# The opening of a two-problem sliding-window attention kernel: Q and K of the first quarter of x computed block by block

## The chip, the cores and the metric

The kernel runs on one core of one Trainium2 chip. The metric is the device time of one execution in microseconds. The kernel before takes 609.3 us (median of three runs, 609.28 to 609.43).

## The reference, cut to what matters

Two independent problems, A and B, have the same shape: x of 2048 x 1024, weights `wqkv` of 1024 x 3072 and `wo` of 1024 x 1024, 32 heads of width 32, each query seeing the last 256 keys. All data are bf16. The results are put side by side.

```python
qkv = (x @ wqkv).reshape(B, S, 3, H, Dh)          # -> q, k, v
scores = einsum(q, k) * Dh ** -0.5                # masked to 0 <= i - j < 256
o = einsum(softmax(scores), v)
out = o.reshape(B, S, D) @ wo
```

## The kernel before

TensorE needs x with its columns on the partitions. Most of x is transposed by DMA on its way in. The first quarter of A's x (512 rows, four blocks of 128) comes in plain rows, and TensorE transposes it: eight 128x128 transposes to a block, into a bank of PSUM, from which ScalarE copies the first half and VectorE the second half into `xT`. The eight column tiles of x are the eight steps (`ct`) over which a projection accumulates.

The loads of the opening, in the order of issue (the first on ScalarE's queue, the others on SyncE's):

```python
load_wqk(0, 0, nc.scalar)                      # Q weights of the first head group
for a in range(QB):
    nc.sync.dma_start(out=xrow[a], in_=problems[0][0][a * P:(a + 1) * P, :])
    if a == 1:
        load_wqk(0, 1, nc.sync)                # K weights
load_wv(0, 0, CT, nc.sync)
new_x(0, 1)
load_x(0, 1)                                   # the next quarter, transposed by DMA
# ... cut
```

TensorE's part of the opening. `keep_warm` issues filler matmuls on zeros, so that the array's clock is up when the work comes:

```python
warm = ps_proj.tile([P, 512], F32, name="pp")

def keep_warm(n):
    for _ in range(n):
        nc.tensor.matmul(warm[:], lhsT=blank[:, 0:P], rhs=blank[:, 0:512], start=True, stop=True)

keep_warm(6)
flips = [ps_acc.tile([P, 512], F32, name="acc") for _ in range(2)]
# ... cut: a third bank of the score tile, a fourth of ps_acc

def flip(a):                                   # transposes of block a, then the two copies
    # ... cut
    for ct in range(CT):
        nc.tensor.transpose(out=f[:, ct, :], in_=xrow[a][:, ct * P:(ct + 1) * P],
                            identity=ident[:])
    dst = xT[(0, 0)][:, :, a * P:(a + 1) * P]
    half = CT // 2
    nc.scalar.copy(out=dst[:, :half, :], in_=f[:, :half, :])
    nc.vector.tensor_copy(out=dst[:, half:, :], in_=f[:, half:, :])

def first(which, lo):                          # Q (0) or K (1), 256 columns, eight matmuls
    for _, f in qk_steps(0, which, 0, lo, lo + 256, held[which], last=lo > 0):
        f()

flip(0)
keep_warm(4)
flip(1)
keep_warm(3)
first(0, 0)
flip(2)
flip(3)
first(1, 0)
first(0, 256)
first(1, 256)
emit(0, chains[0].size)                        # V of the first two blocks
```

The projections share two PSUM slots (`ps_proj`, `bufs=2`): a new chain (`new_pp`) takes the slot that was used longest ago, and must wait until its contents have been cast to SBUF. The cast of a finished Q or K goes to ScalarE or VectorE, whichever a small model of the engines in the kernel's builder takes to be free first.

Of the kernel before, what the change touches and what calls it, by code (L numbers as in the profile page):

```python
# [9 lines left out]
F32 = mybir.dt.float32  # L10
# [8 lines left out]
P = 128  # L19
# [7 lines left out]
QB = 4  # L27
SLOTS = 4
# [50 lines left out]
def _fast_path(ctx, tc, cfg, problems, outs, consts, certify):  # L79
    nc = tc.nc  # L80
# [36 lines left out]
    ps_st = ctx.enter_context(tc.tile_pool(name="ps_st", bufs=1, space=PSUM))  # L117
    ps_acc = ctx.enter_context(tc.tile_pool(name="ps_acc", bufs=2, space=PSUM))
    ps_proj = ctx.enter_context(tc.tile_pool(name="ps_proj", bufs=2, space=PSUM))
# [6 lines left out]
    blank = top[:].bitcast(BF16)  # L126
# [16 lines left out]
    def load_wqk(g, which, queue, lo=0, hi=CT):  # L143
        pi, t = divmod(g, T)
        queue.dma_start(out=wqk[g][:, lo:hi, which, :],
                        in_=wsrc(pi)[:, lo:hi, which, t * P:(t + 1) * P])
# [18 lines left out]
    def qk_tiles(g):  # L165
        if g not in qks:
            qks[g] = (qkp.tile([P, S], BF16, name="qT"), qkp.tile([P, S], BF16, name="kT"))
        return qks[g]

    def by_columns(out, lo, hi, lhsT, rhs, start, stop):  # L170
        if whole[0]:
            nc.tensor.matmul(out[:, lo:hi], lhsT=lhsT, rhs=rhs, start=start, stop=stop,  # L172
                             skip_group_check=True)
            return
        for c in range(0, P, 32):
            nc.tensor.matmul(out[c:c + 32, lo:hi], lhsT=lhsT[:, c:c + 32], rhs=rhs, start=start,  # L176
                             stop=stop, tile_position=(0, c), skip_group_check=True)
# [4 lines left out]
    def add_or(dst):  # L182
        def f():
            nc.vector.tensor_tensor(out=top[:], in0=top[:], in1=dst.bitcast(I32),
                                    op=ALU.bitwise_or)
        side.append((COST["or"], f, False))

    def evacuate(out, in_, engines=("act", "dve")):
        if clock.evacuate(engines) == "act":
            nc.scalar.copy(out=out, in_=in_)  # L190
        else:
            nc.vector.tensor_copy(out=out, in_=in_)

    def new_pp():
        clock.chain()
        return ps_proj.tile([P, 512], F32, name="pp")

    def qk_steps(g, which, k, lo=0, hi=512, st_=None, last=True):
        pi = g // T
        st_ = {} if st_ is None else st_  # L200
        steps = []
        for ct in range(CT):
            def f(ct=ct):
                if "pp" not in st_:
                    st_["pp"] = new_pp()
                by_columns(st_["pp"], lo, hi, wqk[g][:, ct, which, :], xT[(pi, k)][:, ct, lo:hi],
                           ct == 0, ct == CT - 1)
                clock.pe += NS_MM * (hi - lo) / 512.0
                if ct == CT - 1 and last:
                    dst = qk_tiles(g)[which][:, k * 512:(k + 1) * 512]  # L210
                    evacuate(dst, st_["pp"][:])
                    add_or(dst)
            steps.append((NS_MM * (hi - lo) / 512.0, f))
        return steps
# [192 lines left out]
    def emit(now, budget):  # L407
        done = 0.0
        while (current or chains) and done < budget - 0.5 * (current[0][0] if current else NS_MM):
            if not current and not start_chain(now):  # L410
                break
            ns, f = current.pop(0)
            f()
            done += ns
            if side and (clock.dve < clock.pe + 100.0 or len(side) > 8):
                run_side()
# [129 lines left out]
    load_wqk(0, 0, nc.scalar)  # L546
    for a in range(QB):
        nc.sync.dma_start(out=xrow[a], in_=problems[0][0][a * P:(a + 1) * P, :])
        if a == 1:
            load_wqk(0, 1, nc.sync)  # L550
    load_wv(0, 0, CT, nc.sync)
    new_x(0, 1)
# [8 lines left out]
            new_wv(1)  # L561
            load_wv(1, 0, CT, nc.sync)

    warm = ps_proj.tile([P, 512], F32, name="pp")

    def keep_warm(n):
        for _ in range(n):
            nc.tensor.matmul(warm[:], lhsT=blank[:, 0:P], rhs=blank[:, 0:512], start=True, stop=True)  # L568

    keep_warm(6)  # L570
    flips = [ps_acc.tile([P, 512], F32, name="acc") for _ in range(2)]
    flips = [f[:] for f in flips]
    flips.append(ps_st.tile([P, 4, SLOTS, P], F32, name="st")[:, 0].rearrange("p a q -> p (a q)"))
    flips.append(None)
    held = [{}, {}]

    def flip(a):
        if a == 3:
            flips[a] = ps_acc.tile([P, 512], F32, name="acc")[:]
        f = flips[a].bitcast(BF16).rearrange("p (ct q) -> p ct q", q=P)  # L580
# [5 lines that stand above are left out]
        nc.scalar.copy(out=dst[:, :half, :], in_=f[:, :half, :])  # L586
        nc.vector.tensor_copy(out=dst[:, half:, :], in_=f[:, half:, :])

    def first(which, lo):
        for _, f in qk_steps(0, which, 0, lo, lo + 256, held[which], last=lo > 0):  # L590
            f()

    flip(0)
    keep_warm(4)
    flip(1)
    keep_warm(3)
    first(0, 0)
    flip(2)
    flip(3)
    first(1, 0)  # L600
    first(0, 256)
    first(1, 256)
    emit(0, chains[0].size)

    sealed = first_use(G - 1, NQ - 1, 0)
    for now in range(END):
# [3 lines left out]
        while due and due[0][0] <= now:  # L610
            _, pg, pk = due.pop(0)
# [14 lines left out]
    while due:  # L626
        _, pg, pk = due.pop(0)
# [132 lines left out]
def kernel(  # L760
# [48 lines left out]
    with tc.manual_schedule():  # L809
        with ExitStack() as fctx:  # L810
            _fast_path(fctx, tc, cfg, problems, outs, consts, [reduce_bits, decide])
# [40 lines left out]
```

## Time and profile before

| | before |
|---|---|
| median time | 609.3 us |
| span of the profiled run | 607.6 us |
| TensorE busy | 98% |
| TensorE's share of the chain that ended last | 96% |
| first V matmul, first scores | 11.99, 13.83 us |

Two ways of reading matter here. The chain that ended last is followed backwards from the last instruction, at each step to whatever released it; an engine with 96% of it sets the time. The timeline lists instructions by their start, with repeats of one kind merged into one line ("x8"); in brackets is the idle time of that engine before the line, and what ended it. A merged line hides the pauses inside it, so a line that lasts longer than its matmuls should is a sign of a wait. The lines themselves are in the prediction.

### The profile page before, as it was taken

Reading aid. Unit: us, or ns where it says so; the run is one execution under the profiler, and the core shown is the slowest. Engines: PE = TensorE matmul, PEld = TensorE weight load, DVE = VectorE, ACT = ScalarE, POOL = GpSimd, SP = SyncE. Lnnn points to the kernel's source line nnn. Section 1 sums busy time; section 2 is a strip of 40 time slices with the busy share of each in tenths; the row PEclk is TensorE's granted clock in tenths of the full one; section 3 lists DMA queues with packets and bytes.
Section 4 is the critical chain, followed back from the end, with each engine's and each line's share of the span. In section 5 each row is a group of like instructions: output and inputs, shape, how many; then the busy total and the mean of one; then the engine's idle time right before and its main releaser. Section 6 shows DMA issues by size and latency. Waiting matters only on the chain.

```text
span 607.6 us, 28768 instructions
## 1 busy us (share of the span) xinstructions
PE 593.6 (98%) x12786; PEld 344.3 (57%) x12838; DVE 468.4 (77%) x1199; ACT 441.1 (73%) x376; POOL 326.3 (54%) x630
## 2 busy tenths in 40 slices
PE   8999999999999999999999999999999999999996
PEld 6555466656655756564556756655455665545443
DVE  1677889898898898897888887898888887897200
ACT  3778887788888887877778877777776777785332
POOL 0565666665666666556555565555555655554000
PEclk9999999999999999999999999999999999999999
DMA  9833110111015501442111100112021040113222
GB/s 234 182 92 89 37 38 3 38 38 39 3 38 90 114 14 30 82 101 77 38 37 38 38 4 8 33 37 81 2 68 34 4 106 21 55 58 120 72 79 64
DMA packets 86802, 35.47 MB, mean 58 GB/s; under 512 B 65552, under 2 KB 86160, under 8 KB 86672
## 3 DMA queue, kind: packets, MB, share of 16 engines
q1 hardware_dynamic: 85632, 33.31, 22.2%
q8 instruction: 102, 1.67, 1.2%
q10 hardware_dynamic: 1040, 0.26, 0.2%
q14 instruction: 28, 0.23, 0.1%
HBM read 17.83 MB, written 8.39 MB: 43 GB/s over the span
## 4 chain that ended last, share of the span: by engine, by line
PE 96%; ACT 2%; issue 1%; DMA 1%; ACTq 0%
PE pp L176 44%; PE pp L172 28%; PE acc L513 13%; PE st L451 10%; ACT pt L459 1%; DMA oT<-in_A_x_dram 1%; PE acc L582 0%; PE pp L568 0%; ACT kT L190 0%; ACT vt L190 0%; PE st L582 0%; ACT osb L190 0%; PE pp L805 0%; ACTq L190 0%
## 5 line engine op out<-in xcount | busy, mean ns | idle before, releaser
L459 ACT ACTIVATE pt<-st 128x2048 bf16<-128x2048 f32 x180 | 338.0, 1878 | 91.6 <-PE st L451 73.5
L471 POOL TENSOR_SCALAR_AFFINE_SELECT pt<-pt 128x512 bf16<-128x512 bf16 x224 | 154.5, 690 | 145.7 <-ACT pt L459 143.1
L467 POOL TENSOR_SCALAR_AFFINE_SELECT pt<-pt 128x512 bf16<-128x512 bf16 x256 | 179.2, 701 | 85.8 <-ACT pt L459 85.8
L524 DVE RECIPROCAL rinv<-acc 128x128 f32<-128x128 f32 x128 | 122.0, 953 | 57.0 <-PE acc L513 56.4
L176 PE MATMUL pp<-xT,wqk 128*32 128x512 bf16 x2712 | 163.1, 379 | 0.0
L481 DVE TENSOR_TENSOR both<-pt 128x512 bf16<-128x512 bf16 x224 | 137.1, 651 | 0.0
L176 PEld LDWEIGHTS <-wqk 128*32 128x32 bf16 x2712 | 69.3, 97 | 54.2 <-issue 0.4
L172 PE MATMUL pp<-xT,wqk 128*128 128x512 bf16 (+1 forms) x323 | 76.7, 369 | 4.1 <-issue 2.4
L176 PE MATMUL pp<-wv,xT 128*32 128x256 bf16 x2436 | 75.9, 273 | 0.0
L451 PE MATMUL st<-qT,kT 32*128 32x384 bf16 (+2 forms) x1488 | 71.5, 269 | 0.1
L176 PEld LDWEIGHTS <-xT 128*32 128x32 bf16 x2436 | 63.8, 97 | 6.2
L529 DVE STREAM_SHUFFLE wide<-rinv 128x128 f32<-128x128 f32 x256 | 64.6, 298 | 0.0
L513 PE MATMUL acc<-pt,vt 128*32 128x128 bf16 (+1 forms) x2160 | 63.3, 239 | 0.0
L172 PE MATMUL pp<-wo_sb,oT 128*128 128x512 bf16 (+1 forms) x269 | 59.3, 373 | 1.3 <-issue 0.9
L451 PEld LDWEIGHTS <-kT 32*128 32x128 bf16 x1488 | 22.2, 92 | 64.5 <-issue 63.3
L190 ACT CAST osb<-pp 128x512 bf16<-128x512 f32 (+1 forms) x52 | 30.0, 577 | 39.1 <-PE pp L172 24.4
L531 DVE TENSOR_TENSOR oT<-acc,wide 128x256 bf16<-128x256 f32 x128 | 54.3, 425 | 4.4
L176 PE MATMUL pp<-wo_sb,oT 128*32 128x512 bf16 x952 | 55.6, 379 | 0.0
L172 PEld LDWEIGHTS <-wqk 128*128 128x128 bf16 x362 | 33.4, 98 | 37.0 <-issue 6.8
L172 PE MATMUL pp<-wv,xT 128*128 128x256 bf16 x415 | 50.9, 273 | 1.4 <-ACT kT L190 0.6
L513 PEld LDWEIGHTS <-vt 128*32 128x32 bf16 x2160 | 35.9, 96 | 26.4 <-issue 24.1
L172 PEld LDWEIGHTS <-xT 128*128 128x128 bf16 x415 | 38.9, 98 | 12.0 <-issue 6.1
(46 smaller groups left out, 386.5 us busy)
## 6 DMA issues: line engine op xcount, KB each, us to landing
out_dram<-osb SPq DMA_DIRECT2D x63, 128.0 KB, 1.8
wqk<-in_B_wqkv_dram SPq DMA_DIRECT2D x32, 128.0 KB, 2.5
wqk<-in_A_wqkv_dram SPq DMA_DIRECT2D x24, 128.0 KB, 2.7
wo_sb<-in_A_wo_dram SPq DMA_DIRECT2D x16, 128.0 KB, 2.2
wv<-in_B_wqkv_dram SPq DMA_DIRECT2D x16, 128.0 KB, 2.8
wo_sb<-in_B_wo_dram SPq DMA_DIRECT2D x16, 128.0 KB, 2.4
oT<-in_A_x_dram SPq DMA_DIRECT2D x4, 256.0 KB, 5.4
wv<-in_A_wqkv_dram SPq DMA_DIRECT2D x2, 512.0 KB, 5.9
```

The lines of the kernel that those rows point to most:

```text
L172: nc.tensor.matmul(out[:, lo:hi], lhsT=lhsT, rhs=rhs, start=start, stop=stop, skip_group_check=True)
L176: nc.tensor.matmul(out[c:c + 32, lo:hi], lhsT=lhsT[:, c:c + 32], rhs=rhs, start=start, stop=stop, tile_position=(0, c), skip_group_check=True)
L190: nc.scalar.copy(out=out, in_=in_)
L451: nc.tensor.matmul(st[:, r, a:b, :], lhsT=kT[32 * r:32 * r + 32, j * P:(j + 1) * P], rhs=qT[32 * r:32 * r + 32, q * P:(q + b - a) * P], st ...
L459: nc.scalar.activation(out=pt[:, :, :n, :].rearrange("p r a q -> p r (a q)"), in_=st[:, :, :n, :].rearrange("p r a q -> p r (a q)"), func= ...
L467: nc.gpsimd.affine_select(out=blk, in_=blk, pattern=[[0, 4], [1, P]], compare_op=ALU.is_ge, fill=0.0, base=0, channel_multiplier=-1)
L471: nc.gpsimd.affine_select(out=blk, in_=blk, pattern=[[0, 4], [-1, P]], compare_op=ALU.is_gt, fill=0.0, base=0, channel_multiplier=1)
L481: nc.vector.tensor_tensor(out=both[:, :, h, :], in0=pts[s0][:, :, a0, :], in1=pts[s1][:, :, a1, :], op=ALU.add)
L513: nc.tensor.matmul(acc[32 * r:32 * r + 32, o:o + w_], lhsT=lhsT, rhs=src[:, r, :, :], start=(x == 0), stop=(x == len(moves) - 1), tile_pos ...
L524: nc.vector.reciprocal(out=rinv[:], in_=acc[:, 2 * P:3 * P])
L529: nc.vector.stream_shuffle(out=wide[:, h * P:(h + 1) * P], in_=rinv[:], mask=[16 * h] * 32)
L531: nc.vector.tensor_tensor(out=oTs[(pi, k)][:, t, (p % 2) * 256:(p % 2 + 1) * 256], in0=acc[:, 0:256], in1=wide[:], op=ALU.mult)
```

## The change

The intent is to start Q and K as soon as there is a block to work on, rather than at 7.56 us, and to use that work in place of fillers. Each block, once transposed, is followed by its own 128 columns of Q and K. K's weights must then come earlier, so their load moves ahead of block 1. The fillers write into a bank of the score tile, no longer into a projection slot, and there are two fewer.

```diff
-        if a == 1:
+        if a == 0:
             load_wqk(0, 1, nc.sync)
@@
-    warm = ps_proj.tile([P, 512], F32, name="pp")
+    spare = ps_st.tile([P, 4, SLOTS, P], F32, name="st")[:].rearrange("p r a q -> p r (a q)")
+    warm = spare[:, 1]
@@
-    def first(which, lo):
-        for _, f in qk_steps(0, which, 0, lo, lo + 256, held[which], last=lo > 0):
-            f()
+    def first(a):
+        for which in range(2):
+            for _, f in qk_steps(0, which, 0, a * P, (a + 1) * P, held[which], last=a == QB - 1):
+                f()
 
     flip(0)
-    keep_warm(4)
+    keep_warm(3)
+    first(0)
     flip(1)
-    keep_warm(3)
-    first(0, 0)
+    keep_warm(2)
     flip(2)
+    first(1)
     flip(3)
-    first(1, 0)
-    first(0, 256)
-    first(1, 256)
+    first(2)
+    first(3)
     emit(0, chains[0].size)
```

(The third transposition bank is `spare[:, 0]`, as before under another name.)

More of the change, by code (lines that the diff above doesn't have):

```diff
@@ L562, in _fast_path @@
             load_wv(1, 0, CT, nc.sync)
-    warm = ps_proj.tile([P, 512], F32, name="pp")
+    spare = ps_st.tile([P, 4, SLOTS, P], F32, name="st")[:].rearrange("p r a q -> p r (a q)")
+    warm = spare[:, 1]
     def keep_warm(n):
         for _ in range(n):
-            nc.tensor.matmul(warm[:], lhsT=blank[:, 0:P], rhs=blank[:, 0:512], start=True, stop=True)
+            nc.tensor.matmul(warm, lhsT=blank[:, 0:P], rhs=blank[:, 0:512], start=True, stop=True)
     keep_warm(6)
@@ L572, in _fast_path @@
     flips = [f[:] for f in flips]
-    flips.append(ps_st.tile([P, 4, SLOTS, P], F32, name="st")[:, 0].rearrange("p a q -> p (a q)"))
+    flips.append(spare[:, 0])
     flips.append(None)
```

## The prediction

> **What bounds the kernel now.** I read the page first: busy time by engine, then the chain of work that ended last.
>
> ```profile
> PE 593.6 (98%) x12786; PEld 344.3 (57%) x12838; DVE 468.4 (77%) x1199; ACT 441.1 (73%) x376; POOL 326.3 (54%) x630
> ...
> PE 96%; ACT 2%; issue 1%; DMA 1%; ACTq 0%
> PE pp L176 44%; PE pp L172 28%; PE acc L513 13%; PE st L451 10%; ACT pt L459 1%; DMA oT<-in_A_x_dram 1%; PE acc L582 0%; PE pp L568 0%; ACT kT L190 0%; ACT vt L190 0%; PE st L582 0%; ACT osb L190 0%; PE pp L805 0%; ACTq L190 0%
> ```
>
> TensorE is the bound; the other engines have room. The one DMA in the chain is the first block of x (1%), so the chain runs from that load through TensorE to the end. The change touches only the opening, some 14 of 607.6 us, so I read that from the timeline: start, length, engine, work, and in brackets what ended the idle time.
>
> ```profile
> 1.31 2.74 PE L568 MATMUL pp<-top 128*128 128x512 bf16 x6 [1.31 <-DVE ones L783]
> ...
> 4.34 1.04 PE L582 MATMUL acc<-ident,oT 128*128 128x128 bf16 x8 [0.29 <-DMA oT<-in_A_x_dram]
> ...
> 5.17 1.11 PE L568 MATMUL pp<-top 128*128 128x512 bf16 x4
> 5.42 0.59 ACT L586 COPY xT<-acc 128x512 bf16<-128x512 bf16 x1 [2.84 <-PE acc L582]
> 6.04 0.42 DVE L587 COPY xT<-acc 128x512 bf16<-128x512 bf16 x1 [4.73 <-ACT xT L586]
> ...
> 6.26 0.62 PE L582 MATMUL acc<-ident,oT 128*128 128x128 bf16 x8
> ...
> 6.72 0.81 PE L568 MATMUL pp<-top 128*128 128x512 bf16 x3
> ...
> 7.56 1.06 PE L172 MATMUL pp<-xT,wqk 128*128 128x256 bf16 x8
> ...
> 9.35 2.81 PE L172 MATMUL pp<-xT,wqk 128*128 128x256 bf16 x24
> ...
> 11.32 0.59 ACT L190 CAST qT<-pp 128x512 bf16<-128x512 f32 x1 [1.14 <-PE pp L172]
> ...
> 11.99 1.91 PE L172 MATMUL pp<-wv,xT 128*128 128x256 bf16 x16
> 12.19 0.59 ACT L190 CAST kT<-pp 128x512 bf16<-128x512 f32 x1 [0.29 <-PE pp L172]
> ...
> 13.83 0.40 PE L451 MATMUL st<-qT,kT 32*128 32x384 bf16 x8
> ```
>
> L568 are filler matmuls on zeros that hold the clock up; L582 transposes a 128-row block of x; ScalarE, then VectorE, copy half of it each to xT; L172 are the projections. Two starts matter: V at 11.99 and the first scores at 13.83. After V has started I see no wait of TensorE for a load in the first 40 us: the waits view there lists loads only for the raw x blocks. A later V means a later end by as much.
>
> Even before, TensorE's slack in this stretch is small. From the filler at 5.17 to V at 11.99 (6.82 us) it issues 7 fillers (one per 0.216, the first 0.30: 1.59), 24 transposes (one per 0.056, with a start-up of 0.01: 1.35) and 32 projection matmuls (one per 0.109: 3.49), in all 6.43. Idle is about 0.37: 0.15 for block 1 to land, 0.19 for ScalarE's copy of it, 0.03 for VectorE's half.
>
> **What the Trainium skill says.**
> - "TensorE: Matmul & The Clock Gate", Part 1: the clock is halved until the array has been busy for a window of some 3.4 us, then warm matmuls start every N/2.4 ns + 2.5. The trace agrees: fillers start every 0.43 us at first and every 0.216 from about 5.5 us; transposes go from 0.107 to 0.056. The profile's table by stretch gives a granted clock of 1.00 throughout and doesn't show this.
> - The same page, "Back-to-back issue gap": weight-load and matmul pairs with N=128 sustain about 81 ns each. Here it differs: eight 128-column transposes, each with its own weights, take from 6.26 to 6.72, 0.057 each. I use 0.056.
> - "PSUM — Partial Sum Buffer", "PSUM bank collisions raise a hardware error": two engines may not touch one bank and quadrant at once, reads included. The trace shows the consequence: VectorE's copy starts 0.03 after ScalarE's ends (5.42+0.59, then 6.04), so a block takes 1.04 us from first to last copy.
> - "DMA: Bandwidth & Descriptors", "Queues, rings and completion order": each DMA engine consumes a ring in order. The transfer view agrees at the granularity of these loads: issue plus time to landing gives block 0 at 4.30, Q weights (ScalarE's queue) 5.44, block 1 at 6.22, K weights 7.32, blocks 2 and 3 at 8.00 and 8.73.
>
> **The change part by part.**
> The comparison of instruction orders says that only the opening changes. ScalarE loses the cast of the first kT and VectorE gains it; TensorE has 60 rows more (32 matmuls and 32 weight loads more for Q and K, two fillers with their loads fewer). Behind V all engines carry the same operations in the same order.
>
> *Loads.* K weights go ahead of block 1. Between 5.44 and 7.32 both were delivered, 1.88 us, K taking 1.10 of it. Swapped: K weights land at about 6.5, block 1 at about 7.3; blocks 2 and 3 stay.
>
> *Fillers.* 13 become 11, and behind block 0 there are 5 instead of 7: -0.43 us. They now use a bank of the score tile, so Q and K take the two projection slots; V still takes Q's slot, as before.
>
> *Arithmetic.* 32 matmuls of 256 columns (0.109) become 64 of 128 (0.056): 3.58 for 3.49, +0.09.
>
> *Waits.* I step the new order through with the trace's intervals: a copy starts 0.26 after the last transpose starts; ScalarE 0.59, VectorE 0.42; a waiting matmul starts 0.05 after its copy ends. Times are starts of the first matmul.
> 1. Transposes of block 0 at 4.34, three fillers 5.17 to 5.90. ScalarE's copy ends 6.00: Q of block 0 at 6.06, **idle 0.15**. Its four steps last until 6.28; VectorE's half ends 6.46: **idle 0.24**. Q done 6.74; K (weights 6.5, just in time) done 7.19.
> 2. Block 1 lands at 7.3: transposes at 7.35, **idle 0.16**, done 7.80. Copies 8.00 to 8.59 and 8.62 to 9.05.
> 3. Two fillers to 8.24; transposes of block 2 to 8.68, copied 8.88 to 9.93. Q of block 1: four steps, until 8.91; VectorE's half free at 9.10: **idle 0.19**. Q and K done 9.77.
> 4. Transposes of block 3 to 10.22, copied 10.42 to 11.01 and 11.04 to 11.46. Q and K of block 2 from 10.22 to 11.12 without a wait. Q of block 3 at 11.12, four steps, until 11.34; VectorE's half free at 11.52: **idle 0.18**. Last Q matmul starts 11.69, last K matmul 12.13; TensorE free at 12.19.
> 5. V needs Q's slot. Before, the last Q matmul was eight 256-column K matmuls ahead of the end, and the cast ended at 11.91, just before V. Now only eight of 128 columns lie between. Cast of qT from 11.94 to 12.53, V at 12.58: **idle 0.39**.
>
> *Sum.* Idle is 0.15+0.24+0.16+0.19+0.18+0.39 = 1.31 where it was 0.37: +0.94. With -0.43 and +0.09: **+0.60**. V starts at 12.58 instead of 11.99, scores at 14.42 instead of 13.83. kT, on VectorE, is ready at about 13.1, under V's 1.84 us of matmuls, so its move costs nothing. The intended gain, Q and K at 6.06 instead of 7.56, is real but goes into gaps: the blocks' landings and copies set the pace, and useful work is spread out rather than shortened.
>
> **The rivals.**
> - *The filled gaps win.* Had every wait on a copy a cover, the saving would be at most the fillers and the old idle time less the extra arithmetic: 0.43+0.37-0.09 = 0.7, or 608.6. For it: the first projections start 1.5 us earlier. Against: in step 4 nothing but Q and K of block 3 is left behind the last copy, and V waits for Q's cast. A milder form, with block 1 landing near 7.1 or the cast handed over faster, gives 609.6.
> - *Narrow matmuls pay for weight loads.* At the skill's 81 ns the 64 would take 1.6 us more; some falls into the gaps, so 611. For it: these loads read Q and K weights from another layout. Against: the transposes' 0.056 with the same 128x128 loads.
> - *The clock falls back.* More gaps, two fillers fewer. An estimate: one window of 3.4 us at half speed costs some 1.7 us, 611.6. Against: idle before 9.1 adds up to 0.74 in the 3.4 us since 5.7, no gap over 0.24.
> - *K weights arrive late.* If they landed at 6.9, the stall would only move from block 1's transposes to K's; block 1 lands at 7.3 anyway. About zero.
> - *The delay is swallowed later.* TensorE would have to wait there for something that doesn't move with it. The next block of x lands at 13.95 and is used at 15.92, so there is nothing to swallow.
>
> **Range and chances.** 609.3 + 0.6 = 609.9 us. The landing of block 1 carries 0.15 either way, V's wait 0.2, repeats 0.1; the long tail is on the slow side (clock, weight loads). Range 609.3 to 610.6. Two per cent is 12 us; the stretch changed lasts some 10, and nothing behind it changes. Faster 0.01, within 2% 0.98, slower 0.01.
>
> **What would show it.** In the timeline after: Q matmuls at 6.06 (four, then a gap to 6.5); transposes of block 1 at about 7.35, released by the DMA; gaps near 9.0 and 11.4; V at about 12.6, behind the cast of qT; scores at about 14.4; the span longer by the same 0.6. 128-column projections every 0.056, not 0.081. The chain still TensorE. I am wrong if V starts before 12.0, if block 1 lands by 6.9, if matmuls behind 6 us show cold intervals, or if the scores shift and the span doesn't.

## The result, and the profile after

The changed kernel took 610.14 us in the median (609.52 to 610.54, six runs), the kernel before 609.37 (609.18 to 610.27, six runs, the first three of which gave the 609.3 above). The ratio is 1.0008 with a 95% interval from 0.9995 to 1.0021. A ratio here is the mean time of one kernel's fast runs over that of the other's of the same rounds, so it isn't quite the ratio of the medians quoted. By the runs alone the two kernels are the same within 2%, and even the sign is not certain. The profile is sharper.

The page after, its busy times and the chain that ended last:

```profile
PE 593.9 (98%) x12816; PEld 344.9 (57%) x12868; DVE 469.0 (77%) x1200; ACT 440.6 (72%) x375; POOL 326.3 (54%) x630
...
PE 96%; ACT 2%; issue 1%; DMA 1%; ACTq 0%
```

TensorE has 30 matmuls more and otherwise the picture is the same. The timeline of the opening after (L569 are the fillers, L583 the transposes, L587 and L588 the two copies, L190 and L192 the casts):

```profile
4.29 1.03 PE L583 MATMUL acc<-ident,oT 128*128 128x128 bf16 x8 [0.23 <-DMA oT<-in_A_x_dram]
...
5.11 1.19 PE L569 MATMUL st<-top 128*128 128x512 bf16 x3
...
6.14 1.14 PE L172 MATMUL pp<-xT,wqk 128*128 128x128 bf16 x16
...
7.23 0.62 PE L583 MATMUL acc<-ident,oT 128*128 128x128 bf16 x8
...
7.89 0.58 ACT L587 COPY xT<-acc 128x512 bf16<-128x512 bf16 x1 [1.95 <-PE acc L583]
...
8.51 0.42 DVE L588 COPY xT<-acc 128x512 bf16<-128x512 bf16 x1 [2.11 <-ACT xT L587]
...
8.57 1.25 PE L172 MATMUL pp<-xT,wqk 128*128 128x128 bf16 x16
...
10.10 2.13 PE L172 MATMUL pp<-xT,wqk 128*128 128x128 bf16 x32
...
11.81 0.58 ACT L190 CAST qT<-pp 128x512 bf16<-128x512 f32 x1 [0.93 <-PE pp L172]
...
12.26 0.69 DVE L192 CAST kT<-pp 128x512 bf16<-128x512 f32 x1 [0.92 <-PE pp L172]
12.45 1.91 PE L172 MATMUL pp<-wv,xT 128*128 128x256 bf16 x16 [0.23 <-ACT qT L190]
...
14.29 0.40 PE L451 MATMUL st<-qT,kT 32*128 32x384 bf16 x8
```

Q starts at 6.14 instead of 7.56, yet V starts at 12.45 instead of 11.99 and the first scores at 14.29 instead of 13.83: 0.46 us later. The bracket behind V names the reason nearest to it: TensorE stood waiting for the cast of qT. (The bracket says 0.23 because it counts from the modelled end of the last K matmul. This document counts idle time from start to start: V starts 0.446 behind the last K matmul, where a 128-column matmul is followed after 0.056, so the wait is worth 0.39.) Even a merged line shows pauses: sixteen projections of 128 columns last 1.14 or 1.25 us, against 1.06 where nothing interrupts them (an experiment below has that line).

What the delay becomes later can be read by pairing the 180 groups of score matmuls of the two traces: the first is 0.46 late, the last 0.46, and every one between within a few hundredths. The last matmul of the kernel is 0.46 late too (602.36 instead of 601.89). The span is 0.64 longer; the other 0.18 comes behind the last matmul, where the last store took 3.1 us to land instead of 2.9.

### The profile page after: what moved, and what is told of

Read it like the earlier page. It is cut to its first block, busy times and chain, and to the rows that moved or that the text cites. A ratio compares the mean times of both kernels' runs of the same rounds, so it can differ in the third digit from the quotient of the medians.

```text
span 608.3 us, 28827 instructions
## 1 busy us (share of the span) xinstructions
PE 593.9 (98%) x12816; PEld 344.9 (57%) x12868; DVE 469.0 (77%) x1200; ACT 440.6 (72%) x375; POOL 326.3 (54%) x630
## 4 chain that ended last, share of the span: by engine, by line
PE 96%; ACT 2%; issue 1%; DMA 1%; ACTq 0%
PE pp L176 44%; PE pp L172 28%; PE acc L513 13%; PE st L451 10%; ACT pt L459 1%; DMA oT<-in_A_x_dram 1%; PE acc L583 0%; PE st L569 0%; ACT kT L190 0%; ACT vt L190 0%; ACT qT L190 0%; PE st L583 0%; ACT osb L190 0%; PE pp L807 0%; ACTq L190 0%
## 5 line engine op out<-in xcount | busy, mean ns | idle before, releaser
L190 ACT CAST osb<-pp 128x512 bf16<-128x512 f32 (+1 forms) x52 | 30.0, 576 | 39.1 <-PE pp L172 24.4
```

The source lines that it names most:

```text
L190: nc.scalar.copy(out=out, in_=in_)
```

## The experiments

Ten kernels were run, in three groups on the chip; each had five runs, beside nine of the kernel before for each group. All results were correct. All verdicts on the time are "same" with intervals of about 0.13% to either side, so the readings below come from the profiles. Each profile is one execution. For a fair comparison, the table gives when the transposes of block 1 start, when V starts, and the distance between them: the landing of the loads differs from run to run, and everything behind block 1 moves with it.

| kernel | block 1 | V | distance | scores | span | median (before in the same group) |
|---|---|---|---|---|---|---|
| before | 6.26 | 11.99 | 5.73 | 13.83 | 607.6 | 609.37 |
| after | 7.23 | 12.45 | 5.22 | 14.29 | 608.3 | 610.14 (609.37) |
| r_after | 7.21 | 12.43 | 5.22 | 14.27 | 608.4 | 610.21 (609.70) |
| e1_loads_only | 7.62 | 13.34 | 5.73 | 15.19 | 609.1 | 610.87 (610.11) |
| e2_order_only | 8.16 | 13.37 | 5.21 | 15.21 | 609.1 | 610.48 (610.11) |
| e3_qk_spare | 7.07 | 11.89 | 4.83 | 13.74 | 608.2 | 610.09 (610.11) |
| e4_no_fill | 7.62 | 13.28 | 5.66 | 15.12 | 609.1 | 610.89 (610.11) |
| e5_two_banks | 7.33 | 12.18 | 4.85 | 14.02 | 608.2 | 610.00 (609.70) |
| e6_both | 7.34 | 11.79 | 4.45 | 13.63 | 607.5 | 609.68 (609.70) |
| e7_x_first | 6.64 | 13.95 | – | 15.79 | 609.7 | 610.98 (609.70) |
| e8_x_first_fill | 5.64 | 11.40 | – | 13.24 | 607.5 | 609.77 (609.51) |
| e9_both_fill | 7.14 | 11.61 | 4.46 | 13.45 | 607.2 | 609.48 (609.51) |

Between before and after, block 1 comes 0.97 us later and the distance is 0.51 shorter: together they are the 0.46 by which V is late.

My theory was the prediction's sum: the landing of block 1, the two copies in series and V's wait for the cast of qT cost more than the fillers saved. The rivals were that the loads' order is free, that the wait for the cast only hides another, that the copies' series is not what opens the gaps, and that the clock makes the difference.

**The changed kernel again (r_after).** No edit.

> The changed kernel once more, beside the others, to see how much of its opening repeats. The runs so far have block 0 of x landing anywhere from 4.0 to 4.6 us. My theory: V starts 5.1 to 5.3 us behind the first transpose of block 1, wherever that falls (5.22 in the first profile; 5.73 in the kernel before), and the time is 0.3 to 0.9 us over before. Rival (the difference is chance): another distance, or a time under before.

From the timeline of its opening:

```profile
5.04 0.93 PE L569 MATMUL st<-top 128*128 128x512 bf16 x3
...
5.92 1.29 PE L172 MATMUL pp<-xT,wqk 128*128 128x128 bf16 x16
...
7.21 0.62 PE L583 MATMUL acc<-ident,oT 128*128 128x128 bf16 x8
...
12.43 1.91 PE L172 MATMUL pp<-wv,xT 128*128 128x256 bf16 x16 [0.23 <-ACT qT L190]
```

The distance came out the same to 0.01 us, and the time again above before: ratio 1.0012 (0.9998 to 1.0025). The opening repeats behind block 1. Ahead of it the three fillers were shorter here (0.93 us instead of 1.19) and the projections waited longer (1.29 instead of 1.14), with no effect on V; the section on the prediction comes back to this. The total repeats less well: in this profile TensorE lost a further 0.35 us near 260 us, in one group of eight matmuls (the one against the constant ones) that lasted 0.62 us instead of 0.28, with nothing named as a cause.

**The load order alone (e1_loads_only).** The kernel before, with one line changed:

```diff
-        if a == 1:
+        if a == 0:
             load_wqk(0, 1, nc.sync)
```

> The kernel before, with only the K weights' load moved ahead of block 1 of x; TensorE's order unchanged. My theory (the landings of the blocks set the pace of the opening): block 1 lands at about 7.2 instead of 6.2 us, its transposes start at 7.23 instead of 6.26, and nothing behind them is early, so V starts at about 12.95 (before 11.99), the first scores at 14.8, and the time is 0.9 to 1.0 us over before, some 610.4. Rival (the order of the loads is free, the change's cost lies in the narrow matmuls and copies alone): V stays within 0.1 us of 11.99.

The timeline of its block 1:

```profile
7.62 0.62 PE L582 MATMUL acc<-ident,oT 128*128 128x128 bf16 x8 [1.40 <-DMA oT<-in_A_x_dram]
...
13.34 1.91 PE L172 MATMUL pp<-wv,xT 128*128 128x256 bf16 x16
```

The mechanism was as expected: TensorE waits 1.40 us for block 1, and V follows at the same 5.73 us as in the kernel before. The size wasn't, since in this run all the loads landed 0.3 to 0.4 us later than in the profile after (block 0 at 4.57 us instead of 4.24, block 1 at 7.57 instead of 7.19). So the order of loads is not free, and in the old order of work it is pure loss.

**The order of work alone (e2_order_only).** The changed kernel, with that line put back:

```diff
-        if a == 0:
+        if a == 1:
             load_wqk(0, 1, nc.sync)
```

> The changed kernel with the loads in the order of before (block 1 ahead of the K weights). My theory: the K matmuls of block 0, second in the queue, wait until 7.36 us for their weights, block 1's transposes start at 7.8 although block 1 landed at 6.2, and every later step moves by that: V at about 13.0 (after 12.45), 0.5 to 0.6 us over after, 1.0 over before. So the two halves of the change each lose alone and are worth something only together. Rival (the early K weights only delay block 1): V comes before 12.45.

```profile
7.70 0.62 PE L172 MATMUL pp<-xT,wqk 128*128 128x128 bf16 x8 [0.33 <-DMA wqk<-in_A_wqkv_dram]
...
8.16 0.61 PE L583 MATMUL acc<-ident,oT 128*128 128x128 bf16 x8
```

K of block 0 waits for its weights, which landed at 7.66, and block 1's transposes follow at 8.16 although block 1 had landed at 6.53. V comes 1.4 us later than in the kernel before, more than the 1.0 expected because the weights landed 0.3 us later than in the profile of before. Each half of the change is a loss alone (1.35 and 1.38 us, of which some 0.3 is the later landings of these two runs); together they lose less than either.

**V's wait for the cast (e3_qk_spare).** Q and K of the opening get two banks of a pool of their own, which is closed before the score tile takes its place:

```diff
+    opening = ExitStack()
+    ps_open = opening.enter_context(tc.tile_pool(name="ps_open", bufs=1, space=PSUM))
+    spare = [ps_open.tile([P, 512], F32, name=f"spare{i}")[:] for i in range(4)]
+    for which in range(2):
+        clock.chain()
+        held[which]["pp"] = spare[2 + which]
@@ (behind first(3))
+    opening.close()
+    ps_st = ctx.enter_context(tc.tile_pool(name="ps_st", bufs=1, space=PSUM))
```

(`ps_st` is no longer opened further up, and the third transposition bank and the fillers use `spare[0]` and `spare[1]`.)

A first build with Q and K in slices of the one score tile was given up before any run. By my reading of its waits, K's last block would have waited for Q's cast; no run shows this.

> The changed kernel with Q and K of the opening accumulated in two banks of their own (banks that the score tile takes afterwards), so that V takes a projection slot nobody is reading; everything else the same. My theory: V no longer waits for the cast of qT and starts right behind the last K matmul, at about 12.06 instead of 12.45 us; scores at about 13.9 instead of 14.29 (kT and qT are cast long before), the span 0.39 shorter than after. It would then stand within 0.1 us of before. Rival (the wait only moves: the scores wait for kT or qT instead): V at 12.06 but scores still at 14.2 or later.

```profile
11.65 0.59 ACT L189 CAST qT<-spare 128x512 bf16<-128x512 f32 x1 [0.93 <-PE spare L171]
...
11.89 1.91 PE L171 MATMUL pp<-wv,xT 128*128 128x256 bf16 x16
...
13.74 0.40 PE L450 MATMUL st<-qT,kT 32*128 32x384 bf16 x8
```

V now starts while the cast of qT is still running, with no idle time in its bracket. The distance is 4.83, 0.39 below after, which is just what the wait was worth, and the scores follow V as closely as before: the wait did not move elsewhere. The first scores are 0.09 ahead of the kernel before. The time doesn't tell (ratio 0.9999): in this profile the last matmul started within 0.02 us of that of before, and the span was 0.6 longer, all of it behind that matmul.

**The fillers (e4_no_fill).** The changed kernel without the fillers behind blocks 0 and 1:

```diff
     flip(0)
-    keep_warm(3)
     first(0)
     flip(1)
-    keep_warm(2)
     flip(2)
```

> The changed kernel without the five fillers behind blocks 0 and 1 (the first six stay). If the fillers only fill gaps (my step that counted fewer fillers as 0.43 us saved was then no real saving): Q of block 0 starts at 6.0, the transposes of block 1 still at 7.23 when it lands, V within 0.1 us of 12.45. If they hold up the clock (rival): matmuls after 6 us start every 0.107 instead of 0.056 us for some time and V comes 0.5 to 1.7 us later. If they cost their full time: V 0.4 earlier or more.

```profile
5.93 1.90 PE L172 MATMUL pp<-xT,wqk 128*128 128x128 bf16 x16 [0.67 <-ACT xT L587]
...
7.62 1.06 PE L583 MATMUL acc<-ident,oT 128*128 128x128 bf16 x8
8.47 0.95 PE L583 MATMUL st<-ident,oT 128*128 128x128 bf16 x8
```

Sixteen projections last 1.90 us instead of 1.14, and eight transposes 1.06 instead of 0.62: TensorE starts a 128-column matmul every 0.107 us until about 9.2 us, instead of every 0.056. Block 1 had landed at 7.18 and waited for TensorE until 7.62. V comes 0.83 later than after. The rival was right: in the profile after full rate came near 5.9 us, without the five fillers over 3 us later. They help to bring the clock up, and in this profile that was worth more than they cost. My reading of two of them as 0.43 us of work saved had left this out. (One of the five runs took 609.93 us, the other four 610.72 to 611.18; the profile is of one of the four. Whether the clock came up earlier in the short one isn't shown.)

**The two copies (e5_two_banks).** The changed kernel with four transposes of a block in each of two banks, so that the two engines read different banks:

```diff
-            nc.tensor.transpose(out=f[:, ct, :], in_=xrow[a][:, ct * P:(ct + 1) * P],
+            nc.tensor.transpose(out=fs[ct // half][:, ct % half, :],
+                                in_=xrow[a][:, ct * P:(ct + 1) * P],
@@
-        nc.scalar.copy(out=dst[:, :half, :], in_=f[:, :half, :])
-        nc.vector.tensor_copy(out=dst[:, half:, :], in_=f[:, half:, :])
+        nc.scalar.copy(out=dst[:, :half, :], in_=fs[0][:, :half, :])
+        nc.vector.tensor_copy(out=dst[:, half:, :], in_=fs[1][:, :half, :])
```

(The banks come from `ps_acc` and from a pool as in e3; Q and K stay in the projection slots.)

> The changed kernel with each block's transposes put into two banks, four to each, so that ScalarE's and VectorE's copies no longer have to follow each other; the rest the same. My theory (the serial pair of copies makes the gaps inside Q of blocks 1 and 3, 0.19 and 0.18 us in the profile after): both gaps vanish, V starts 4.8 to 4.9 us behind the first transpose of block 1 instead of 5.22, still after waiting 0.39 for the cast of qT; the time 0.37 under after. Rival (the gaps come from something else, such as the hand-over of the copy): the distance stays over 5.1.

```profile
7.76 0.59 ACT L586 COPY xT<-spare 128x512 bf16<-128x512 bf16 x1 [2.21 <-PE spare L583]
...
7.98 0.43 DVE L587 COPY xT<-spare 128x512 bf16<-128x512 bf16 x1 [2.16 <-PE spare L583]
...
8.66 1.06 PE L171 MATMUL pp<-xT,wqk 128*128 128x128 bf16 x16
...
12.18 1.91 PE L171 MATMUL pp<-wv,xT 128*128 128x256 bf16 x16 [0.23 <-ACT qT L189]
```

VectorE is now released by TensorE and not by ScalarE, the copies overlap, and sixteen projections last 1.06 us. The distance fell by 0.37 to 4.85, as expected, and V still waits for the cast.

**Both together (e6_both).** The two edits in one kernel, the fillers in a projection slot.

> The two-bank copies and the banks of their own for Q and K together. If the two waits are separate terms of the sum, they add: V 4.4 to 4.5 us behind the first transpose of block 1, about 11.7 us with a landing as in the first profile, 0.3 us under before. If they overlap, 4.6 or more.

```profile
7.34 0.61 PE L586 MATMUL spare<-ident,oT 128*128 128x128 bf16 x8
...
11.79 1.91 PE L171 MATMUL pp<-wv,xT 128*128 128x256 bf16 x16
```

The distance is 4.45: 5.22 less 0.39 less 0.37 is 4.46. The two waits are separate terms and add. V starts at 11.79, 0.20 before the kernel before, although here the clock came up late (the first projections started every 0.107 us) and block 1, landed at 7.04, waited for TensorE until 7.34.

**Loads of x first (e7_x_first).** An attempt at something better: blocks 0 and 1, then Q weights, blocks 2 and 3, then K weights; two-bank copies; Q in pieces as the blocks come, K in one piece last.

```diff
-    load_wqk(0, 0, nc.scalar)
     for a in range(QB):
-        nc.sync.dma_start(out=xrow[a], ...)
-        if a == 0:
-            load_wqk(0, 1, nc.sync)
+        queue = nc.scalar if a == 1 else nc.sync
+        queue.dma_start(out=xrow[a], ...)
+        if a == 1:
+            load_wqk(0, 0, nc.sync)
+    load_wqk(0, 1, nc.sync)
@@
-    keep_warm(3); first(0); flip(1); keep_warm(2); flip(2); first(1); flip(3); first(2); first(3)
+    keep_warm(2); flip(1); keep_warm(2); first(0, 0, 256); flip(2); flip(3); keep_warm(1)
+    first(0, 256, 384); first(0, 384, 512); first(1, 0, 512)
```

(Shortened: the calls stand on lines of their own in the kernel. Cut: `flip` as in e5, the pool of banks as in e3, and `first`, which here takes Q or K and a range of columns.)

> An attempt at a version that beats both: the loads in the order x0, x1, Q weights, x2, x3, K weights; copies from two banks; Q in pieces of 256, 128 and 128 columns as the blocks come, K last in one piece of 512 columns, behind Q's cast. By the landings seen (0.7 us for a block of x, 1.1 for a set of weights, the last of them at 8.6 to 8.7): Q starts at about 6.2, its last piece ends at 9.2, K's eight 512-column matmuls of 0.216 end at about 11.0 and V follows without a wait, 1.0 us earlier than before; the time about 0.9 under before, if the clock is up by 6 us. If not, V at 11.5 or later.

```profile
4.96 1.03 PE L584 MATMUL acc<-ident,oT 128*128 128x128 bf16 x8 [0.91 <-DMA oT<-in_A_x_dram]
...
8.35 1.91 PE L171 MATMUL pp<-xT,wqk 128*128 128x256 bf16 x8
```

It failed. Eight projections of 256 columns last 1.91 us, where before eight took 1.06: the clock was down, until about 10.4 us. Block 0 was in flight together with block 1 and landed at 4.92, and TensorE stood still for about 1 us after the first six fillers (0.91 by the bracket). The five times fall into two groups, 609.63 and 609.84, and 610.98 to 611.46; the profile is of the slower group. That the clock was up in the other is likely but not shown.

**The same with the clock in mind (e8_x_first_fill), and the two-bank version likewise (e9_both_fill).** Eight fillers instead of six ahead of block 0; in e8 none between blocks 0 and 1 and three behind.

```diff
-    keep_warm(6)
+    keep_warm(8)
@@ (e8 alone)
     flip(0)
-    keep_warm(2)
     flip(1)
-    keep_warm(2)
+    keep_warm(3)
```

> The x-first version with eight fillers instead of six ahead of block 0, none between blocks 0 and 1, three behind block 1. In the x-first profile TensorE stood still from 3.8 to 4.96 us and the 256-column matmuls started every 0.214 until 10.2 us: the clock was down. If that alone cost it the gain: with TensorE busy from 1.3 us on, matmuls go at full rate from 5 to 6 us, the last Q piece ends near 9.2, K's eight near 11.0, V follows at 10.8 to 11.2, scores near 13.0, time 0.8 to 1.1 us under before in most runs. Rival (the step-through of the x-first order is wrong in its landings or copies): V after 12 with full-rate matmuls.

> The two-bank version with Q and K in their own banks, with eight fillers instead of six ahead of block 0. Block 1's landing, at 7.0 to 7.3, is the pace here, so a clock that is up earlier gains nothing unless it was late: V again 4.4 to 4.5 us behind the first transpose of block 1, near 11.7, time within 0.2 us of the version with six.

```profile
6.80 1.04 PE L171 MATMUL pp<-xT,wqk 128*128 128x256 bf16 x8
...
11.40 1.91 PE L171 MATMUL pp<-wv,xT 128*128 128x256 bf16 x16
...
13.24 0.40 PE L450 MATMUL st<-qT,kT 32*128 32x384 bf16 x8
```

In e8's profile, shown here, the matmuls ran at full rate and the scores start 0.59 us before those of the kernel before; this carried to the last matmul (0.59). V came at 11.40, a little past the 11.2 that I had allowed; block 0 was still transposed at half rate, from 4.82, which may be why. But the five times run from 609.28 to 610.95, and the ratio to before is 1.0009 (0.9995 to 1.0022). e9 put V at 11.61 with a distance of 4.46, as expected, and its last matmul 0.38 ahead of that of before; its times run from 608.95 to 610.49, ratio 1.0004. So both of these versions beat both kernels in the opening of their profiled run, as e3 and e6 did, and none of them beats the kernel before in time that these runs could show.

## Why the prediction was right, and where it wasn't

The predicted 609.9 us held: 610.14 measured. The direction held in the profiles, with 0.46 us of delay in the opening where the sum said 0.60; the times alone don't settle it.

- *The bound, and that a delay in the opening reaches the end.* Right. All 180 score groups and the last matmul moved by 0.46. The next quarter of x landed at 15.37 in the profile after and was used at 16.38, so nothing swallowed it. In e4, e8 and e9 too the shift of the first scores stood unchanged at the end; in r_after, e3, e5 and e6 pauses of 0.1 to 0.4 us in mid-run came on top.
- *Loads.* Right: K weights at 6.51 (predicted 6.5), block 1 at 7.19 (7.3). e1 shows that this alone costs the old order about as much as block 1 comes later.
- *Arithmetic.* Right: narrow matmuls start every 0.056 us; the 64 take 3.56 us against 3.51 of the 32 wide ones (a pause of 0.02 included), +0.05 for a predicted +0.09. The rival that they would go at 81 ns is out.
- *V's wait for the cast of qT.* 0.39 predicted, 0.39 measured, and removed by e3 at just that gain.
- *The gaps from the serial copies.* 0.19 and 0.18 predicted for blocks 1 and 3, 0.19 and 0.18 measured, and removed by e5.
- *Fillers, and the gaps ahead of block 1: wrong in this profile.* The prediction took two fillers fewer as "-0.43 us", at 0.216 each. The five left took 1.46 us (5.11 to 6.14 and two of 0.216), the seven before 1.59: a saving of 0.13. The clock came up only near 5.9 us in this run, so the first two fillers took 0.43 and 0.39. For the same reason they ran on over ScalarE's copy of block 0, and the predicted gaps of 0.15, 0.24 and 0.16 were 0.00, 0.09 and 0.11.
- *The sum in their place.* Idle: 0.00 + 0.09 + 0.11 + 0.19 + 0.18 + 0.39 = 0.96 where it was 0.36, so +0.60; fillers -0.13; arithmetic +0.05; together +0.52. Block 0 landed 0.06 earlier than in the profile of before: +0.46 for V.
- *Why the two misses cancel.* It is not luck. Block 1's transposes can't start before it lands, so time that fillers take before then is time that TensorE doesn't have to wait. r_after shows it: there the clock came up near 5.3 us (the first filler behind block 0 took 0.33, the next 0.22), the five fillers took 1.19 us (0.40 less than the seven), the gaps ahead of block 1 were 0.12, 0.24 and 0.16, as the prediction had them, and V still came 5.22 us behind block 1. So the step took the moment at which the clock comes up from one trace, and that moment differs from run to run.
- *The rival of the falling clock.* Put aside in the prediction by counting idle time. It didn't decide this change, but e4 and e7 show that it lay near: in e4's profile five fillers fewer cost 0.83 us.

What stays open: the medians differ by 0.77 us in one comparison and 0.51 in the other, the opening by 0.46. The rest is within the scatter of single runs, and the scatter has at least four sources that the traces show: the landing of block 0 (4.0 to 4.6 us in kernels that issue it alike), the moment the clock comes up, single pauses of up to 0.4 us mid-run, and the last store.

## What to carry to other kernels

Moving work earlier gains nothing where what follows still waits for the last arrival and its chain of copies: add up the idle time that the new order opens, wait by wait, before counting the idle time that it fills. Cutting a chain into pieces also takes away the work that stood between its end and the reuse of its buffer; here that uncovered 0.39 us of a cast. Fillers dropped ahead of an arrival that sets the pace can't be counted as work saved: in r_after 0.40 us less of them turned into waiting for block 1, and in e4, without all five, the real matmuls ran at half rate for 3 us longer.

## What the Trainium skill lacked or had wrong

- "TensorE: Matmul & The Clock Gate". Part 1 gives a warm-up budget of about 3.4 us, in a window that runs freely, and has the change vary by about 500 ns either way. Here, after a first filler at 1.31 us, it varied more: full rate came between 4.8 us (e3_qk_spare) and 6.7 (e6_both) in kernels with the same first six fillers, and after a standstill of about 1 us behind them only at about 10.4 (e7_x_first). Part 4 says that the full rate doesn't engage for transposes; here they ran at it, one every 0.056 us, once it was up, and in e1_loads_only the change came in the middle of eight transposes, at about 4.9 us. "Back-to-back issue gap" has 81 ns for a sustained 128-column matmul with its weight load; here 32 in a row, each with its own load, took 0.056 us each (e6_both, 10.01 to 11.79).
- "PSUM — Partial Sum Buffer", "PSUM bank collisions raise a hardware error", says that two engines must not be in one bank and quadrant at once. It doesn't name the price of keeping to it: here VectorE's 0.42 us to each block, 0.37 us of the opening, which a second bank took away (e5_two_banks).
- "DMA: Bandwidth & Descriptors" doesn't say how much the landing of the first loads varies from run to run: block 0, 256 KB issued at 0.80 us, landed between 4.03 and 4.63 us in kernels that issue it alike.
- I found no page that has TensorE's pauses in mid-run for which the profile names no cause (0.35 us near 260 us in r_after), which limit how small a gain the time alone can show. Their cause stays open here.
